# A fused attention and FFN kernel: two preparations moved behind the start of the FFN, one batch's RMS regrouped, and the last output tile split

## The chip, the cores and the metric

The kernel runs on one core of one Trainium2 chip. A core has a matrix engine (TensorE, PE in the profile), a vector engine (VectorE, DVE), a scalar engine (ScalarE, ACT), a general engine (GpSimd, POOL), and a queue engine (SyncE, SP) that mostly issues DMAs. Each engine has an instruction queue of its own; semaphores order them. The metric is the device time of one execution in microseconds, and of several executions the median.

## What is computed

Attention with routing by clusters feeds a gated FFN. Cut to what matters:

```python
batch, n_heads, seq, head_dim = (4, 8, 768, 64)      # 16 clusters a head
q_assign = argmax(q_n @ c_n.T); k_assign = argmax(k_n @ c_n.T)
mask   = q_assign[:, None] == k_assign[None, :]
scores = where(mask, q @ k.T / sqrt(D), -1e9)
attn   = softmax(scores) @ v                          # 4 x 8 x 768 x 64
x   = attn.transpose(0, 2, 1, 3).reshape(3072, 512)
xn  = x / sqrt(mean(x * x) + 1e-6) * rms_g
out = (silu(xn @ w_gate) * (xn @ w_val)) @ w_out      # d_ff = 1536
```

The FFN works on tokens, and a token's 512 features come from all eight heads of a batch. So the FFN of a batch can begin once the attention of its last head is done.

## The kernel before

**Slots, steps and pairs.** A slot is one head of one batch; there are 32. The scores of a slot are 768 x 768, held with keys on partitions, and are made in 9 steps of 512 columns (`NCH`), so the attention is a loop of 288 steps. Slots 8b to 8b+7 are batch b. Two neighbouring heads form a pair; there are 16, and pair p is used from step 18p on.

**Preparation of a pair** (`prep_parts`) has 13 parts, each put at a step by a table: four transpose groups on PE (`t_group`, three fp32 transposes each, copied from PSUM to `qk32` by DVE or by ACT), casts into the operand `aug` on POOL (`casts`), the product with the centroids on PE (`assign`), five DVE instructions that make a one-hot mask from it (`oh_tr` to `oh_back`), four small DMAs on SP that put the mask rows into `aug` (`place`), and a cast of v on POOL (`casts_v`). The mask rows make the scores of other clusters very negative, so no mask is applied later. `aug` and the cast v have three sets of buffers. The tables count from `base`, which for most pairs is step 18(p-2): there pair p-3, whose set pair p takes, has been used up, and pair p's own slots begin 36 steps later.

**Scores, exp, PV.** `score_chunk` makes the scores on PE and ACT takes the exp into `pT`. Before the FFN begins (the wide stage) one chunk is three steps long: 1536 columns, one exp, two PSUM buffers of three banks. Afterwards a chunk is one step of 512 columns. The PV product of a slot (`pv_group`, six groups of six matmuls) follows in steps 2 to 7 of the next slot. It accumulates in one PSUM buffer, `acc`. In step 8 of that slot `pv_norm` divides by the sums on DVE and writes the head's columns of `x`. The next slot's PV can't begin before.

**RMS of a batch** (`rms_parts`) has 14 parts for a batch's two halves of three token tiles each: the sums of squares of three tiles (`sumsq`, on ACT or on DVE, tile `jk`), the inverse root on POOL (`inv`, tile `ir`), the scaling of three tiles on DVE (`norm`, tile `xn`), and with the last of these a transposing DMA on SP into `xnT`. The parts' steps are counted from 72(b+1), the first step after batch b's last slot.

**The FFN** (`ffn_piece`) is cut into pieces, one to a step: of each unit of 128 hidden columns a gate product (`gp`, L382, then tanh on ACT and a product on DVE), a value product (`vp`, L382, then `gvT` on DVE) and, from the second half of a batch on, a quarter of an output tile (`dp`, L411: three matmuls of 512 columns; after four of them the eviction `ob`, L417 or L419, and the store). `LAG` is the number of steps by which the FFN of a batch starts behind the batch's last slot. After step 288 come `LAG` steps with FFN pieces and the rest of the last head, and then FFN pieces alone, with evictions on ACT.

**Order.** It is written out by hand: nothing reorders an engine's instructions. In each step the code emits the score chunk, one FFN piece, the evictions still pending but one, the PV group or the normalisation, and then the extras of that step: first the RMS parts, then preparation parts, loads and weight loads, as `at` registered them.

```python
for step in range(NT):
    score_chunk(slot, j)
    ffn_next(...)
    flush(1)
    if slot > 0 and 2 <= j < 2 + ST:
        pv_group(slot - 1, j - 2)
    if slot > 0 and j == 2 + ST:
        pv_norm(slot - 1)
    extras(step)
```

Of the kernel before, what the change touches and what calls it, by code (L numbers as in the profile page):

```python
# [8 lines left out]
F32 = mybir.dt.float32  # L9
# [10 lines left out]
def kernel(  # L20
# [12 lines left out]
    nc = tc.nc  # L33
    B, H, S, D = q.shape
    NC = centroids.shape[1]
    DM, DF = moe_w_gate.shape
    P = 128
# [3 lines left out]
    FC = DF // P  # L41
# [3 lines left out]
    NCH = ST * S // CH  # L45
# [7 lines left out]
    out_v = out.rearrange("(b p t) d -> b p t d", b=B, t=ST)  # L53
# [7 lines left out]
    ffn = ctx.enter_context(tc.tile_pool(name="ffn", bufs=2))  # L61
# [6 lines left out]
    wide = ExitStack()  # L68
    WCH = 3
    late = {}  # L70
    LAG = 33
    FFN0 = H * NCH + LAG

    ctx.enter_context(tc.manual_schedule())
# [12 lines left out]
    def load_pair(pi):  # L87
        for kind in range(3):
            load_part(pi, kind)
# [65 lines left out]
    wo = const.tile([P, FC, DM], BF16, name="wo")  # L155
# [25 lines left out]
    def prep_parts(pi):  # L181
        st = pi % NSET
        qk32 = [None]
        state = {}

        def t_group(g):
            a, side = divmod(g, 2)
            if g == 0:
                qk32[0] = prep.tile([P, 4, HS], F32, name="qk32", tag="qk32")
            tp = t_tile("tp")  # L190
            src = loads[pi][side]
            for i in range(TH):
                nc.tensor.transpose(tp[:, i * P:(i + 1) * P], src[:, a, i * P:(i + 1) * P], ident_f)  # L193
            dst = qk32[0][:, g, :]
            on_dve = (g % 2 == 0 if pi == 0 else g > 0 if pi == 1 else pi < 9 or g % 2)
            if on_dve:
                nc.vector.tensor_copy(dst, tp)  # L197
            else:
                nc.scalar.copy(dst, tp)
            state[g] = tp  # L200

        def casts():
            if pi == 0:
                for g in range(4):
                    a, side = divmod(g, 2)
                    for par in range(2):
                        dst = aug[0][a][0:D, side, par * HS:(par + 1) * HS]
                        src = state[g][par * D:(par + 1) * D, :]
                        if g == 3:
                            nc.vector.tensor_copy(dst, src)  # L210
                        else:
                            nc.scalar.copy(dst, src)
                return
            for a in range(2):
                for par in range(2):
                    nc.gpsimd.tensor_copy(aug[st][a][0:D, :, par * HS:(par + 1) * HS],  # L216
                                          qk32[0][par * D:(par + 1) * D, 2 * a:2 * a + 2, :])

        def casts_v():
            v_in = loads[pi][2]  # L220
            nc.gpsimd.tensor_copy(vbf[st][:, :, :, 0:D],  # L221
                                  v_in[:, :, :].rearrange("p a (t d) -> p a t d", d=D))

        def assign():
            h0 = 2 * (pi % NP)
            sp = t_tile("sp")
            for j in range(4):
                side, a = divmod(j, 2)
                nc.tensor.matmul(sp[32 * j:32 * j + 32, :], lhsT=cbd[:, h0 + a, :, :].rearrange("p c r -> p (c r)"),  # L229
                                 rhs=qk32[0][:, 2 * a + side, :], start=True, stop=True,  # L230
                                 tile_position=(0, 32 * j))
            state["sp"] = sp

        def oh_tr():
            tr = prep.tile([P, HS], F32, name="tr", tag="tr")
            nc.vector.transpose(tr, state["sp"])
            state["tr"] = tr[:, :].rearrange("p (n c r) -> p n r c", c=NC, r=2)

        def oh_max():
            mx = small.tile([P, TH * 4, 2], F32, name="mx", tag="mx")  # L240
            nc.vector.tensor_reduce(mx, state["tr"], axis=AX, op=ALU.max)
            state["mx"] = mx

        def oh_cmp():
            oh = prep.tile([P, HS], BF16, name="oh", tag="oh")
            nc.vector.tensor_tensor(oh[:, :].rearrange("p (n c r) -> p n r c", c=NC, r=2), state["tr"],
                                    state["mx"].unsqueeze(3).to_broadcast([P, TH * 4, 2, NC]), op=ALU.is_ge)
            state["oh"] = oh

        def oh_scale():  # L250
            oh = state["oh"]
            nc.vector.tensor_scalar(oh[0:64, :], oh[0:64, :], scalar1=1.0, scalar2=MASK,
                                    op0=ALU.subtract, op1=ALU.mult)

        def oh_back():
            ohT = prep.tile([P, HS], BF16, name="ohT", tag="ohT")
            nc.vector.transpose(ohT, state["oh"])
            state["ohT"] = ohT

        def place():  # L260
            ohT = state["ohT"]
            for a in range(2):
                for side in range(2):
                    r = 32 * (2 * side + a)
                    eng = nc.sync
                    if pi == 0:
                        eng = nc.gpsimd if side else nc.scalar
                    elif pi == 1 and (a or side):
                        eng = nc.gpsimd
                    eng.dma_start(out=aug[st][a][D:KA, side, :].rearrange("c (r n) -> c r n", r=2),  # L270
                                  in_=ohT[r:r + 2 * NC, :])

        return [lambda: t_group(0), lambda: t_group(1), lambda: t_group(2), lambda: t_group(3), casts, assign, oh_tr, oh_max, oh_cmp, oh_scale, oh_back, place, casts_v]


# [51 lines left out]
    def rms_parts(b):  # L327
        st = {}

        def sumsq(t):  # L330
            m, tl = divmod(t, TH)
            if tl == 0:
                st["ss"] = small.tile([P, TH], F32, name="ss", tag="ss")
                st["jk"] = xp.tile([P, 2, DM], BF16, name="jk", tag="jk")
            if tl % 2 == 0:
                nc.scalar.activation(st["jk"][:, 0, :], x_t[b][:, t, :], ACT.Square,  # L336
                                     accum_out=st["ss"][:, tl:tl + 1])
            else:
                nc.vector.scalar_tensor_tensor(st["jk"][:, 1, :], x_t[b][:, t, :], 1.0, x_t[b][:, t, :],
                                               op0=ALU.mult, op1=ALU.mult, accum_out=st["ss"][:, tl:tl + 1])  # L340
# [26 lines left out]
    gvT = {}  # L367
# [3 lines left out]
    def ffn_piece(n, kind, tail, on_act):  # L371
# [27 lines left out]
        elif kind == 2 and half >= 1:  # L399
            hf = half - 1  # L400
            b, m = divmod(hf, 2)
            t = m * TH + fc // 4
            qd = fc % 4
            if qd == 0:
                pool, tag = (ps_pv, "acc") if tail and (fc // 4) % 2 else (late["d"], "d")
                cur["d"] = pool.tile([P, DM], F32, name="dp", tag=tag)
            dp = cur["d"]
            for i in range(3):
                f = qd * 3 + i
                tl = fc // 4  # L410
                nc.tensor.matmul(dp, lhsT=gvT[hf][:, f, tl * P:(tl + 1) * P], rhs=wo[:, f, :],  # L411
                                 start=(f == 0), stop=(f == FC - 1))
            if qd == 3:
                def after():
                    ob = ffn.tile([P, DM], F32, name="ob", tag="ob", bufs=3)
                    if on_act:
                        nc.scalar.activation(ob, dp, ACT.Copy, scale=0.5)  # L417
                    else:
                        nc.vector.tensor_scalar_mul(ob, dp, 0.5)  # L419
                    nc.sync.dma_start(out=out_v[b, :, t, :], in_=ob)  # L420
                pend.append(after)

    def flush(keep=0):
# [19 lines left out]
    def at(step, fn):  # L443
        extra.setdefault(step, []).append(fn)
# [24 lines left out]
    for b in range(B):  # L469
        steps = (9, 9, 10, 11, 12, 13, 15, 19, 19, 25, 26, 27, 28, 29)  # L470
        if b == 0:
            steps = (9, 9, 9, 14, 16, 18, 19, 20, 21, 21, 27, 30, 31, 33)
        for fn, step in zip(rms_parts(b), steps):
            at(H * NCH * (b + 1) + step, fn)
    for pi in range(2, B * NP):
        base = 2 * NCH * (pi - 2) + {2: 10, 3: 5}.get(pi, 0)
        if pi < 9:
            steps = (-8, -5, -3, 0, 1, 2, 4, 5, 6, 7, 9, 9, 10)
        else:
            steps = (-5, -4, -3, -2, 0, 1, 2, 3, 4, 5, 6, 6, 10)  # L480
        for fn, step in zip(prep_parts(pi), steps):
            at(base + step, fn)
        if pi < B * NP - 3:
            at({6: 100, 7: 106}.get(pi, base + 12), lambda pi=pi: load_pair(pi + 3))
    for i, step in enumerate((50, 58, 68, 76, 86, 94, 100, 105, 111, 117, 123, 129)):
        at(step, lambda i=i: w_load(i))
    def extras(step):
# [58 lines left out]
```

## Time and profile before

| what | value |
|---|---|
| time, median of 13 runs | 355.75 us (354.45 to 357.61) |
| the profiled execution | 357.09 us; its span 355.1 us |
| PE busy | 337.2 us, 95% of the span |
| weight loads (PEld) busy | 204.1 us |
| ACT busy | 224.7 us |
| DVE busy | 221.4 us |
| POOL busy | 87.0 us |
| chain that ended last | PE 77%, DVE 9%, ACT 5%, DMA 4% |
| mean of one wide exp (1536 columns) | 1453 ns, 35 of them |
| mean of one narrow exp (512 columns) | 597 ns, 183 of them |
| mean of one fp32 transpose | 287 ns, 192 of them |

The span is measured from the first to the last instruction of one profiled execution; the time of a run includes a little around it. A matmul's duration contains its latency, and matmuls overlap, so the spacing of their starts says what they cost, not their mean. In rows of the timeline the columns are start, duration, engine, line, operation, output and input tiles, and count; brackets give how long the engine was idle just before and what ended the wait. Rows of the windows view give the stretch and its length, then busy microseconds (and counts) of PE, weight loads, DVE, ACT and POOL, then the granted PE clock as a share of full speed, the share of the DMA engines and GB/s.

### The profile page before, as it was taken

To read this page: it belongs to the slowest core of one execution; us is meant where nothing else is said; L and a number is where in the kernel's file an instruction comes from. 1 tells how busy PE (TensorE), PEld (TensorE's weight loads), DVE (VectorE), ACT (ScalarE), POOL (GpSimd) and SP (SyncE) were. 2 spreads that over 40 slices of the span, in tenths; PEclk is the share of its full clock that TensorE was granted. 3 is DMA by queue.
4 is the path that set the end of the run, shared out by engine and by line. 5 is a ranking of instruction groups with operands and counts; after the bars stand their busy time and mean duration, and the time that the engine had idled before them with its cause. 6 is when DMAs were issued, how large, how long until landed. Compare 5 with 4: busy or idle time off the path is not lost.

```text
span 355.1 us, 7433 instructions
## 1 busy us (share of the span) xinstructions
PE 337.2 (95%) x2907; PEld 204.1 (57%) x2939; DVE 221.4 (62%) x449; ACT 224.7 (63%) x383; POOL 87.0 (25%) x122
## 2 busy tenths in 40 slices
PE   8888999799999999999999999999999999999995
PEld 3456666466656565556656565556666555555542
DVE  4657667867575678757474668855545687555630
ACT  3487888787778687767667687767775442323321
POOL 2674565763332123230311224200000110000000
PEclk9999999879999999999999999999999999999999
DMA  7466799689954053071400013130000053000012
GB/s 263 150 196 185 222 224 225 92 125 293 266 128 142 4 173 74 20 202 38 137 35 8 31 41 47 42 74 31 2 30 32 30 77 75 31 30 30 31 59 89
DMA packets 38194, 35.38 MB, mean 100 GB/s; under 512 B 15072, under 2 KB 34960, under 8 KB 38160
## 3 DMA queue, kind: packets, MB, share of 16 engines
q1 hardware_dynamic: 31936, 29.98, 28.0%
q0 software_dynamic: 5984, 4.84, 9.7%
q8 instruction: 23, 0.38, 0.4%
q10 hardware_dynamic: 240, 0.08, 0.1%
q14 instruction: 11, 0.09, 0.1%
HBM read 28.61 MB, written 6.29 MB: 98 GB/s over the span
## 4 chain that ended last, share of the span: by engine, by line
PE 77%; DVE 9%; ACT 5%; DMA 4%; issue 3%; POOL 1%; POOLq 0%; SPq 0%; DVEq 0%; ACTq 0%
PE gp L382 15%; PE vp L382 15%; PE dp L411 15%; PE sc L297 10%; PE acc L311 8%; PE tp L193 5%; PE scw L297 5%; PE sp L229 3%; DVE xn L353 2%; ACT pT L300 2%; DVE qk L197 2%; DMA aug<-ohT 2%; DMA q_in<-in_q_dram 1%; DMA k_in<-in_k_dram 1%; ACT jk L336 1%
## 5 line engine op out<-in xcount | busy, mean ns | idle before, releaser
L300 ACT ACTIVATE pT<-sc 128x512 bf16<-128x512 f32 x183 | 108.0, 597 | 44.4 <-PE sc L297 43.5
L391 DVE SCALAR_TENSOR_TENSOR uu<-th,gp 128x384 f32<-128x384 f32 x96 | 53.0, 552 | 61.8 <-ACT th L387 61.8
L382 PE MATMUL vp<-xnT,wv 128*128 128x384 bf16 x384 | 78.1, 325 | 1.5 <-DVE gvT L397 1.4
L387 ACT ACTIVATE th<-gp 128x384 f32<-128x384 f32 x96 | 47.1, 491 | 49.2 <-PE gp L382 45.0
L382 PE MATMUL gp<-xnT,wg 128*128 128x384 bf16 x384 | 78.1, 325 | 0.0
L311 PEld LDWEIGHTS <-pT 128*128 128x128 bf16 x1152 | 58.5, 98 | 27.3 <-DVE x L321 2.9
L411 PE MATMUL dp<-wo,gvT 128*128 128x512 bf16 x257 | 69.8, 378 | 3.1 <-ACT ob L417 1.5
L297 PE MATMUL sc<-aug 80*128 80x512 bf16 x244 | 69.2, 327 | 0.8 <-ACT pT L300 0.8
L216 POOL CAST aug<-qk 64x768 bf16<-64x768 f32 x60 | 52.1, 868 | 62.0 <-DVE qk L197 51.3
L311 PE MATMUL acc<-vbf,pT 128*128 128x65 bf16 x1152 | 64.1, 195 | 1.9 <-DVE x L321 1.3
L300 ACT ACTIVATE pT<-scw 128x1536 bf16<-128x1536 f32 x35 | 48.9, 1453 | 15.4 <-PE scw L297 15.3
L397 DVE TENSOR_TENSOR gvT<-uu,vp 128x384 bf16<-128x384 f32 x96 | 52.6, 548 | 6.4 <-PE vp L382 0.9
L382 PEld LDWEIGHTS <-wg 128*128 128x128 bf16 x384 | 37.2, 97 | 30.8 <-issue 0.9
L382 PEld LDWEIGHTS <-wv 128*128 128x128 bf16 x384 | 37.1, 97 | 21.1 <-issue 2.6
L297 PEld LDWEIGHTS <-aug 80*128 80x128 bf16 x384 | 33.7, 99 | 22.6 <-issue 9.7
L411 PEld LDWEIGHTS <-gvT 128*128 128x128 bf16 x288 | 27.9, 98 | 27.3 <-issue 2.3
L197 DVE COPY qk<-tp 128x384 f32<-128x384 f32 x47 | 25.9, 554 | 24.7 <-PE tp L193 22.4
L297 PE MATMUL scw<-aug 80*128 80x512 bf16 (+1 forms) x140 | 30.2, 340 | 2.0 <-DMA aug<-ohT 1.4
L221 POOL CAST vbf<-v_in 128x768 bf16<-128x768 f32 x16 | 13.2, 825 | 46.8 <-issue 41.9
L353 DVE SCALAR_TENSOR_TENSOR xn<-x,ir,g_b 128x512 bf16<-128x512 bf16 x24 | 20.1, 850 | 6.6 <-POOL ir L345 6.6
L344 POOL TENSOR_SCALAR ir<-ss 128x3 f32<-128x3 f32 x8 | 1.6, 195 | 88.3 <-ACT jk L336 86.5
L321 DVE TENSOR_TENSOR x<-acc,inv 128x384 bf16<-128x384 f32 x32 | 17.8, 557 | 1.1
(54 smaller groups left out, 202.1 us busy)
## 6 DMA issues: line engine op xcount, KB each, us to landing
q_in<-in_q_dram SPq DMA_DIRECT2D x16, 384.0 KB, 4.6
k_in<-in_k_dram SPq DMA_DIRECT2D x16, 384.0 KB, 5.3
v_in<-in_v_dram SPq DMA_DIRECT2D x16, 384.0 KB, 5.8
out_dram<-ob SPq DMA_DIRECT2D x24, 256.0 KB, 2.0
wg<-in_moe_w_gate_dram POOLq DMA_DIRECT2D x4, 384.0 KB, 5.6
wv<-in_moe_w_val_dram POOLq DMA_DIRECT2D x4, 384.0 KB, 6.5
wo<-in_moe_w_out_dram POOLq DMA_DIRECT2D x4, 384.0 KB, 7.8
aug<-ohT SPq DMA_DIRECT2D x57, 24.0 KB, 2.2
```

Of the source, the lines that this page charges most:

```text
L197: nc.vector.tensor_copy(dst, tp)
L216: nc.gpsimd.tensor_copy(aug[st][a][0:D, :, par * HS:(par + 1) * HS], qk32[0][par * D:(par + 1) * D, 2 * a:2 * a + 2, :])
L297: nc.tensor.matmul(sc[:, o:o + n], lhsT=ag[:, 1, kc * P:(kc + 1) * P], rhs=ag[:, 0, qo:qo + n], start=True, stop=True)
L300: nc.scalar.activation(pts[slot][:, j * CH:(j + nch) * CH], sc[:, :nch * CH], ACT.Exp, scale=scale)
L311: nc.tensor.matmul(acc[:, TORD[g], :], lhsT=pts[slot][:, kc * S + g * P:kc * S + (g + 1) * P], rhs=vb[:, a, TORD[kc], :], start=(kc == 0), ...
L321: nc.vector.tensor_tensor(x_t[b][:, :, h * D:(h + 1) * D], acc[:, :, 0:D], inv.to_broadcast([P, ST, D]), op=ALU.mult)
L353: nc.vector.scalar_tensor_tensor(st["xn"][:, tl, :], x_t[b][:, t, :], st["ir"][:, tl:tl + 1], g_b, op0=ALU.mult, op1=ALU.mult)
L382: nc.tensor.matmul(pt[:, :HS], lhsT=w[:, dc, fc * P:(fc + 1) * P], rhs=xnT[b, m][:, :, dc, :], start=(dc == 0), stop=(dc == DC - 1))
L387: nc.scalar.activation(th, pt[:, :HS], ACT.Tanh, scale=0.5)
L391: nc.vector.scalar_tensor_tensor(uu, th, 1.0, pt[:, :HS], op0=ALU.add, op1=ALU.mult)
L397: nc.vector.tensor_tensor(gvT[half][:, fc, :], uu, pt[:, :HS], op=ALU.mult)
L411: nc.tensor.matmul(dp, lhsT=gvT[hf][:, f, tl * P:(tl + 1) * P], rhs=wo[:, f, :], start=(f == 0), stop=(f == FC - 1))
```

## The change

Four things are changed.

1. Pairs 7 and 8. Their preparation is moved: counted from the first transpose to `casts_v`, pair 7 goes from steps 82 to 100 to steps 102 to 117, and pair 8 from steps 100 to 118 to steps 109 to 124. They also take the tighter table of steps that pairs 9 and up have, and half of their PSUM copies go to ACT as those pairs' do. The loads of pair 10 go from step 106 to 118, those of pair 11 from 120 to 126.
2. RMS of batch 0. Its parts stood at steps 81 to 105 and now stand at steps 81 to 93. Of each half's three sums of squares two were on ACT and one on DVE; for batch 0 it is now one on ACT and two on DVE.
3. `LAG` goes from 33 to 30, so the FFN begins at step 102 instead of 105, the wide stage ends there, and three steps fewer follow the last slot.
4. The last output tile is made in two halves of 256 columns, each with its own PSUM buffer, eviction and store.

```diff
-    LAG = 33
+    LAG = 30
...
-            on_dve = (g % 2 == 0 if pi == 0 else g > 0 if pi == 1 else pi < 9 or g % 2)
+            on_dve = (g % 2 == 0 if pi == 0 else g > 0 if pi == 1 else pi < 7 or g % 2)
...
-            if tl % 2 == 0:
+            if tl == 2 or tl == 0 and b > 0:
                 nc.scalar.activation(st["jk"][:, 0, :], x_t[b][:, t, :], ACT.Square,
                                      accum_out=st["ss"][:, tl:tl + 1])
...
-            if qd == 0:
-                pool, tag = (ps_pv, "acc") if tail and (fc // 4) % 2 else (late["d"], "d")
+            tl = fc // 4
+
+            nh = 2 if n >= NU + FC - 4 else 1
+            qh, nq, N = qd * nh // 4, 4 // nh, DM // nh
+            if qd % nq == 0:
+                pool, tag = (ps_pv, "acc") if tail and (tl + qh) % 2 else (late["d"], "d")
                 cur["d"] = pool.tile([P, DM], F32, name="dp", tag=tag)
-            dp = cur["d"]
-            for i in range(3):
-                f = qd * 3 + i
-                tl = fc // 4
-                nc.tensor.matmul(dp, lhsT=gvT[hf][:, f, tl * P:(tl + 1) * P], rhs=wo[:, f, :],
+            dp = cur["d"][:, 0:N]
+            cols = slice(qh * N, (qh + 1) * N)
+            for i in range(3 * nh):
+                f = (qd % nq) * 3 * nh + i
+                nc.tensor.matmul(dp, lhsT=gvT[hf][:, f, tl * P:(tl + 1) * P], rhs=wo[:, f, cols],
                                  start=(f == 0), stop=(f == FC - 1))
-            if qd == 3:
+            if qd % nq == nq - 1:
...
-                    ob = ffn.tile([P, DM], F32, name="ob", tag="ob", bufs=3)
+                    ob = ffn.tile([P, DM], F32, name="ob", tag="ob", bufs=3)[:, 0:N]
...
-                    nc.sync.dma_start(out=out_v[b, :, t, :], in_=ob)
+                    nc.sync.dma_start(out=out_v[b, :, t, cols], in_=ob)
...
         if b == 0:
-            steps = (9, 9, 9, 14, 16, 18, 19, 20, 21, 21, 27, 30, 31, 33)
+            steps = (9, 9, 9, 10, 11, 12, 13, 14, 15, 16, 18, 19, 20, 21)
...
-        base = 2 * NCH * (pi - 2) + {2: 10, 3: 5}.get(pi, 0)
-        if pi < 9:
+        base = 2 * NCH * (pi - 2) + {2: 10, 3: 5, 7: 17, 8: 6}.get(pi, 0)
+        if pi < 7:
             steps = (-8, -5, -3, 0, 1, 2, 4, 5, 6, 7, 9, 9, 10)
         else:
             steps = (-5, -4, -3, -2, 0, 1, 2, 3, 4, 5, 6, 6, 10)
...
-            at({6: 100, 7: 106}.get(pi, base + 12), lambda pi=pi: load_pair(pi + 3))
+            at({6: 100, 7: 118}.get(pi, base + 12), lambda pi=pi: load_pair(pi + 3))
```

## The prediction

> **What bounds the kernel now.** I read the page's busy times first: PE is busy for 337.2 of 355.1 us, ACT 224.7, DVE 221.4, POOL 87.0. So the kernel is a PE queue, and what counts is where that queue stands still or runs at half clock. The windows of 10 us put the largest loss, after the start, between 60 and 80 us; in windows of 2 us:
>
> ```profile
> 62.00:64.00 2.00, 2.00 (x35) 1.63 (x32) 0.85 (x2) 1.97 (x6) 0.14 (x1) 1.00 0.62 99
> 64.00:66.00 2.00, 1.09 (x13) 0.78 (x12) 1.50 (x2) 2.00 (x2) 1.91 (x4) 1.00 0.23 53
> 66.00:68.00 2.00, 0.86 (x10) 0.49 (x8) 1.97 (x5) 2.00 (x3) 1.94 (x2) 0.98 0.74 55
> 68.00:70.00 2.00, 1.72 (x9) 0.33 (x10) 2.00 (x3) 0.39 (x2) 1.88 (x3) 0.50 0.92 142
> 70.00:72.00 2.00, 2.00 (x23) 1.48 (x22) 1.90 (x6) 0.78 (x1) 1.60 (x2) 0.50 0.92 175
> 72.00:74.00 2.00, 2.00 (x21) 1.33 (x19) 0.22 (x1) 1.79 (x4) 0.49 (x2) 0.50 0.82 80
> 74.00:76.00 2.00, 2.00 (x20) 1.38 (x18) 1.74 (x5) 1.77 (x2) 2.00 (x3) 0.82 0.91 139
> ```
>
> [...]PE works half of 64 to 68 us while DVE is full; then the clock is 0.50 until about 74.7 us. The timeline of this stretch says why (rows of DVE, POOL, PE and ACT):
>
> ```profile
> 60.66 0.69 DVE L339 SCALAR_TENSOR_TENSOR jk<-x 128x512 bf16<-128x512 bf16 x1
> ...
> 64.14 0.88 POOL L345 TENSOR_TENSOR ir<-ir,mhalf 128x3 f32<-128x3 f32 x1
> ...
> 65.06 1.34 DVE L353 SCALAR_TENSOR_TENSOR xn<-x,ir,g_b 128x512 bf16<-128x512 bf16 x1 [0.19 <-POOL ir L345]
> ...
> 66.54 0.56 DVE L321 TENSOR_TENSOR x<-acc,inv 128x384 bf16<-128x384 f32 x1
> ...
> 67.16 0.36 PE L311 MATMUL acc<-vbf,pT 128*128 128x65 bf16 x6 [0.66 <-DVE x L321]
> ...
> 71.22 1.45 ACT L300 ACTIVATE pT<-scw 128x1536 bf16<-128x1536 f32 x1 [2.83 <-PE scw L297]
> ...
> 75.17 2.79 ACT L300 ACTIVATE pT<-scw 128x1536 bf16<-128x1536 f32 x2 [0.23 <-PE scw L297]
> ...
> 78.22 0.81 PE L382 MATMUL gp<-xnT,wg 128*128 128x384 bf16 x4
> ```
>
> The RMS of batch 0 (jk, ir, xn) stands in the DVE queue ahead of the normalisation of slot 8 (66.54). There is one acc buffer, so the PV of slot 9 waits for it (67.16), the score chunk of step 93 queues behind that PV, and ACT is without an exp for 2.83 us. The first FFN matmul comes at 78.22, step 105. From there PE is full: 9.9 of 10 us in nearly every window.
>
> **What the Trainium skill says.** TensorE: Matmul & The Clock Gate, section Architectural detail: ACT and DVE queues are strict FIFO, and on PE only weight loads are pulled ahead. The rows above agree: slot 8's normalisation cannot pass xn. The same page, Part 1: PE falls to half rate after an idle window of about 3.4 us and recovers after a busy one. Here the means of 0.98 and 0.82 put half clock from 67.9 to 74.7 us, two such windows, and half activity was enough to bring it on. SBUF — State Buffer, section Terms: DVE and POOL take a shared port pair exclusively for a whole instruction. An xn of 1.34 us beside 0.74 us for the next one fits, though the trace doesn't prove it.
>
> **The change part by part.** "Step 102" and so on are the kernel's steps; all before step 81 is unchanged, so its times stand.
>
> *RMS of batch 0 (steps 81 to 93 instead of 81 to 105).* DVE's new order after slot 7's normalisation (done 60.63) is jk, jk, transpose of pair 6, xn, xn, xn, jk, jk, and only then slot 8's normalisation; after it xn x3. Only one Square of each half stays on ACT. DVE jk at a pitch of 0.62: 60.66, 61.28, done 61.9. ACT's Square stands behind the exp that ends at 62.40, as before, and is done at 63.0 (before, two were done at 63.77). From there to the first xn took 1.29 us (63.77 to 65.06): first xn at 64.3. Three xn at 0.70 and two jk at 0.62 are 3.35 us, the normalisation 0.78: done at 68.4, or 69.0 if one xn is again 0.6 slower. I take 68.8, so the PV of slot 9 starts at 68.9, where it started at 67.16. PE finishes what stands ahead of it (the chunk of step 90) at 65.3, since the exp of step 84 now ends at 64.3. So PE idles 3.6 us in one piece, and the clock must fall wherever its windows lie.
>
> *Pairs 7 and 8 leave the wide stage.* Before, PE filled part of its waits with their transposes. Now it has chunks and PV alone, and nothing gets ACT further: the step 93 chunk starts at 68.9 + 0.4 (six slow PV matmuls) = 69.3, before at 69.72. From that start the trace takes 1.5 us to the exp at 71.22 and 5.34 from there to the end of the step 99 exp (75.17 + 1.39 = 76.56). So 69.3 + 1.5 + 5.34 = 76.1 at this pace; without transposes, and if the clock recovers one window sooner, 75.2. If the clock never fell: 68.9 + 0.3 + 0.8 + three exps of 1.39 = 74.2. I take 75.8, bounds 74.2 and 77.0 (DVE ops slowed twice by POOL). The first FFN step waits for the last wide exp both times (78.01 before, after 77.96), so it is at 75.8: **2.2 us earlier**.
>
> *What PE must still do then.* The price of a pair's preparation beside the FFN is read from the gp matmuls, one per three steps:
>
> ```profile
> 84.27 0.81 PE L382 MATMUL gp<-xnT,wg 128*128 128x384 bf16 x4
> ...
> 91.44 0.81 PE L382 MATMUL gp<-xnT,wg 128*128 128x384 bf16 x4
> ...
> 97.71 0.81 PE L382 MATMUL gp<-xnT,wg 128*128 128x384 bf16 x4
> ...
> 101.40 0.81 PE L382 MATMUL gp<-xnT,wg 128*128 128x384 bf16 x4
> ```
>
> Nine steps without preparation take 91.44 - 84.27 = 7.17 us (2.39 per three). Nine with pair 9 take 9.96: a pair costs 2.8 us. Of this, 84.27 to 101.40 shows four transpose groups at 6.27 - 4.78 = 1.5, 0.37 each. Pair 7 moves whole (2.8); of pair 8 the two groups of steps 100 and 103 move (0.75, bounds 0.75 to 1.5, as the rest of pair 8 took 1.27 of 2.8 after 78.22). Steps 102 to 104 now have their scores and PV beside the FFN: 2.39 less gp and vp, which in the tail cost (306.85 - 297.12) / 5 - 0.65 = 1.30 us a pair; 1.1 us. Sum **+4.65**, of work that PE did in or beside its waits before. Fewer tail steps by three give nothing: the same FFN pieces run earlier in the same full PE queue.
>
> *Crowding.* Two preparations in steps 102 to 124 instead of one per 18. DVE's share at steps 109 to 113 comes to 5 x 0.37 (uu, gvT) + 2.5 (one-hot chain) + 1.1 (two copies), about 5.5 us, against about 5.5 of PE (5 x 0.8 + 4 x 0.37). Half of the two pairs' copies go to ACT, 0.48 each, which has 3 x 0.60 + 0.49 = 2.3 us of work in three steps of 2.39 plus 1.1 for three groups. I take +0.2, bounds 0 and 1.
>
> *Queues.* On SP the second input transposition (xnT, now step 93 instead of 105) and the loads of pair 9 (step 100) now stand ahead of pair 7's four aug copies (step 113, needed at 126); the loads of pair 10 go from 106 to 118, needed at 139, and land in about 5 us. On POOL the gate and value weight loads go ahead of pair 7's casts. Both cost nothing, with more than 10 us of slack each. FFN weights: the last value piece is issued at step 105, first used near 130.
>
> *Last tile in halves.* The chain ends with
>
> ```profile
> 351.35 0.60 ACT L417 ACTIVATE ob<-dp 128x512 f32<-128x512 f32 x1 [2.04 <-PE dp L411]
> ```
>
> and, in the windows view, the last store's data:
>
> ```profile
> 352.75:353.65 0.90, 0.00 (x0) 0.00 (x0) 0.00 (x0) 0.00 (x0) 0.00 (x0) 1.00 0.75 291
> ```
>
> Eviction of 512 columns takes 0.60; 384 columns (th) 0.49, so 256 about 0.39. The last store moves 291 GB/s for 0.9 us; half of it 0.45. Issue (0.8) and the 1.45 us after the data stay. PE's columns are the same; 24 matmuls of 256 for 12 of 512 cost nothing as long as the weight loads hide. **-0.55**, bounds -0.2 and -0.65.
>
> Sum: -2.2 + 4.65 + 0.2 - 0.55 = **+2.1 us**. The profiled execution took 357.09 us, its span and 2.0 around it; so 359.2 for such a one. It lies 1.3 above the median of 355.75, and I put the change on the median: **357.9 us**.
>
> **Rivals.**
> - *Faster, 353.9.* The DVE stretch does not hold up slot 8. With PE free, the wide stage is ACT's: seven exps of 1.39 (steps 81 to 99) and two Squares of about 0.65 end at 72.0 if the first starts at 61.0 as before; FFN 6.0 earlier, -6.0 + 4.65 - 0.55 = -1.9. It decides from where PV of slot 9 starts: the end of the stage is that start + 5.3 (warm) or + 6.9 (cold), and the break-even end is 78.0 - 4.65 + 0.35 = 73.7, so a start before 66.8 cold, 68.4 warm. For it: Square and ir come 0.8 us earlier than before. Against: five DVE operations in order after 64.3.
> - *No change, 355.5.* PE in the early FFN stage has room (9.47 busy in 90 to 100 us), and more preparation fills it: 2.3 of the 4.65 vanish. Against: pair 9 shows the full 2.8 there.
> - *Slower still, 360.5.* DVE falls behind with two preparations at once and gvT holds the vp buffers (PE waited 0.5 us for it at 99.2 already), five times over.
>
> **How the numbers follow.** Main case 0.60, own range 356.0 to 359.6 (from all low bounds together, +0.2, to most of the high ones, +3.8); faster 0.18; no change 0.12; slower still 0.10. About 0.3% (1.1 us) is what a measurement can tell from none. Faster takes its 0.18 and 0.02 of the others' edges: 0.20; same 0.12 and the low end of the main case, 0.16; slower 0.64. Range 353.8 to 360.2.
>
> **What would show it.** Right: slot 9's PV waits on x until about 69 us, PE clock 0.5 after it, first gp near 76, then gp spaced as around pair 9 twice between steps 102 and 124, last eviction about 0.4 us. Wrong: first gp before 73.5, no clock dip, or gp spacing under 3 us where pairs 7 and 8 are prepared.

## The result and the profile after

The changed kernel takes 361.44 us in the median of 11 runs (358.07 to 365.21), beside 356.33 us (354.39 to 359.05, 48 runs) for the kernel before on the same chip: a ratio of 1.0133 with an interval of 1.0109 to 1.0156. That is slower, as forecast, but 3.5 us more than the forecast and 1.2 us outside its range; 0.6 of the 3.5 us is the kernel before itself, taken as 355.75 in the forecast. The ratios and the table of runs below leave out every run over 1.5% above its kernel's fastest, called slow: of the changed kernel one, at 365.21 us. The profiled execution took 360.57 us, its span is 358.8.

The stretch where the RMS of batch 0 now stands, in the windows view of the kernel after (columns as before):

```profile
64.00:66.00 2.00, 1.63 (x35) 1.24 (x31) 0.58 (x3) 2.00 (x4) 0.64 (x2) 1.00 0.76 121
66.00:68.00 2.00, 0.81 (x4) 0.32 (x4) 1.52 (x2) 2.00 (x3) 2.00 (x3) 1.00 0.12 28
68.00:70.00 2.00, 0.00 (x0) 0.00 (x0) 1.97 (x5) 1.64 (x3) 0.01 (x1) 0.95 0.68 48
70.00:72.00 2.00, 0.80 (x8) 0.53 (x9) 1.31 (x5) 0.00 (x0) 1.31 (x3) 0.50 1.28 206
72.00:74.00 2.00, 2.00 (x23) 1.53 (x22) 1.87 (x3) 0.97 (x1) 2.00 (x3) 0.50 1.09 176
74.00:76.00 2.00, 2.00 (x17) 1.27 (x16) 0.04 (x1) 1.18 (x2) 0.04 (x1) 0.50 1.04 132
76.00:78.00 2.00, 1.23 (x10) 0.58 (x9) 0.71 (x2) 1.66 (x2) 0.00 (x0) 0.84 1.28 194
```

Before, PE worked half of the time from 64 to 68 us; now it does nothing at all from 68 to 70, while DVE is full. Half clock follows again. The timeline of the kernel after names the wait:

```profile
66.47 2.62 DVE L353 SCALAR_TENSOR_TENSOR xn<-x,ir,g_b 128x512 bf16<-128x512 bf16 x3 [1.89 <-POOL ir L345]
...
69.74 0.69 DVE L339 SCALAR_TENSOR_TENSOR jk<-x 128x512 bf16<-128x512 bf16 x1
...
70.58 0.56 DVE L321 TENSOR_TENSOR x<-acc,inv 128x384 bf16<-128x384 f32 x1
...
71.20 0.51 PE L311 MATMUL acc<-vbf,pT 128*128 128x65 bf16 x6 [3.78 <-DVE x L321]
...
73.03 1.45 ACT L300 ACTIVATE pT<-scw 128x1536 bf16<-128x1536 f32 x1 [3.39 <-PE scw L297]
...
78.80 0.81 PE L382 MATMUL gp<-xnT,wg 128*128 128x384 bf16 x4
...
354.33 0.39 ACT L421 ACTIVATE ob<-dp 128x256 f32<-128x256 f32 x1 [0.76 <-PE dp L415]
355.64 0.38 ACT L421 ACTIVATE ob<-dp 128x256 f32<-128x256 f32 x1 [0.92 <-PE dp L415]
```

Three xn and two jk pass ahead of slot 8's normalisation (70.58); the PV of slot 9 waits 3.78 us for it (0.66 before), and ACT is 3.39 us without an exp (2.83 before). The last two rows are the halved output tile.

This profile began badly: from 20 to 30 us its mean clock is 0.73, where the profile before has 1.00, and step 81, whose instructions up to there are unchanged, comes 2.00 us later. So times are best counted from the exp of step 81 (60.95 us before). The table cuts the rest of the span at the first tanh of the FFN, at the seventh, and at the last one in the trace; "half clock" counts stretches of 3.41 us at clock 0.50, before step 81 and then after it; what follows the last matmul of a span is not counted. Rows marked with a label are experiments told below.

| profile | half clock | to first tanh | to seventh | to last | to end | sum |
|---|---|---|---|---|---|---|
| before | 0, 2 | 18.13 | 16.45 | 245.87 | 13.70 | 294.15 |
| before_3 (same kernel) | 0, 0 | 16.18 | 16.44 | 245.89 | 13.71 | 292.22 |
| after | 2, 2 | 16.70 | 18.70 | 247.31 | 13.13 | 295.84 |
| after_3 (same kernel) | 0, 4 | 17.77 | 20.51 | 247.34 | 13.15 | 298.77 |
| warm | 0, 0 | 14.56 | 18.70 | 247.31 | 13.15 | 293.72 |
| norm_first | 0, 2 | 14.01 | 20.51 | 247.32 | 13.13 | 294.97 |
| norm_both | 1, 0 | 11.83 | 18.69 | 247.32 | 13.13 | 290.97 |
| only_rms | 0, 2 | 20.07 | 16.44 | 245.87 | 13.69 | 296.07 |
| no_rms | 0, 2 | 14.41 | 19.51 | 247.31 | 13.13 | 294.36 |
| pair7_wide | 0, 0 | 15.42 | 16.90 | 247.31 | 13.15 | 292.78 |
| both_warm | 0, 0 | 11.83 | 18.69 | 247.31 | 13.14 | 290.97 |

With two stretches after step 81 in each, the change costs 295.84 - 294.15 = 1.7 us. The other 3 us or so of the median are not in this pair of profiles. They are in how often the clock falls, which only many runs show.

### The profile page after: what moved, and what is told of

It is laid out like the page before. It is cut to its first block, busy times and chain, and to the rows that moved or that the text cites. A ratio compares the mean times of both kernels' runs of the same rounds, so it can differ in the third digit from the quotient of the medians.

```text
span 358.8 us, 7459 instructions
## 1 busy us (share of the span) xinstructions
PE 338.9 (94%) x2918; PEld 206.5 (58%) x2951; DVE 219.9 (61%) x449; ACT 225.8 (63%) x386; POOL 85.2 (24%) x122
## 4 chain that ended last, share of the span: by engine, by line
PE 85%; DVE 7%; ACT 3%; DMA 2%; issue 2%; POOL 1%; POOLq 0%; DVEq 0%; ACTq 0%
PE gp L382 17%; PE dp L415 17%; PE vp L382 16%; PE sc L297 11%; PE acc L311 9%; PE scw L297 6%; PE tp L193 5%; PE sp L229 3%; DVE qk L197 2%; ACT pT L300 2%; DVE xn L353 1%; DMA aug<-ohT 1%; ACT ob L421 1%; DVE x L321 1%; DMA c_in<-in_centroids_dram 1%
## 5 line engine op out<-in xcount | busy, mean ns | idle before, releaser
L300 ACT ACTIVATE pT<-sc 128x512 bf16<-128x512 f32 x186 | 109.9, 597 | 45.6 <-PE sc L297 44.7
L415 PE MATMUL dp<-wo,gvT 128*128 128x512 bf16 (+1 forms) x268 | 71.2, 369 | 3.6 <-ACT ob L421 1.9
L297 PE MATMUL sc<-aug 80*128 80x512 bf16 x248 | 70.3, 326 | 1.4 <-ACT pT L300 1.4
L216 POOL CAST aug<-qk 64x768 bf16<-64x768 f32 x60 | 50.3, 838 | 72.5 <-DVE qk L197 64.3
L300 ACT ACTIVATE pT<-scw 128x1536 bf16<-128x1536 f32 x34 | 47.9, 1455 | 18.9 <-PE scw L297 18.7
L415 PEld LDWEIGHTS <-gvT 128*128 128x128 bf16 x300 | 29.2, 98 | 27.1 <-issue 3.1
L197 DVE COPY qk<-tp 128x384 f32<-128x384 f32 x43 | 23.6, 555 | 26.3 <-PE tp L193 25.7
L297 PE MATMUL scw<-aug 80*128 80x512 bf16 (+1 forms) x136 | 31.5, 359 | 2.1 <-POOL ir L345 1.0
```

Source lines behind the costliest of these rows:

```text
L297: nc.tensor.matmul(sc[:, o:o + n], lhsT=ag[:, 1, kc * P:(kc + 1) * P], rhs=ag[:, 0, qo:qo + n], start=True, stop=True)
L300: nc.scalar.activation(pts[slot][:, j * CH:(j + nch) * CH], sc[:, :nch * CH], ACT.Exp, scale=scale)
```

## The experiments

**The same two kernels again.** No edit; two more profiles of each.

> The changed kernel once more. In the first pair of profiles the changed kernel was 3.7 us longer, and 2.0 of that came before step 81, where both run the same instructions; there the PE clock fell to half from 18.6 to 25.4 us in one profile and not in the other. Theory 1 (chance of the clock): this early dip falls on either kernel, so a new profile may lack it, and the change itself is worth about +1.7 us net of it. Theory 2 (the change is worth what the medians say): +4.7 us again, with at least 4 us of it after step 81. Theory 3: the early dip belongs to the changed program and is there again.

> The kernel before once more, against itself: a ratio of 1.000 within about 0.004. Theory 1: its profile has the early dip in some executions too, and is then about 2 us longer before step 81. Theory 3: never an early dip.

> A third look at the changed kernel, for one more profile. If the length of half clock after the wait makes its spread of 358.1 to 365.2 us: this run's time is about 356.7 us, plus 2 us for two stretches of half clock after the wait or 5 for four, plus 0.5 to 2 us if the early dip is there.

> A third look at the kernel before. One of its two profiles had half clock after step 84 (span 355.1), the other none (353.5). By the same account: a span of about 353.1, plus 1.6 us with half clock there, plus 0.5 to 2 us with the early dip.

The changed kernel: 360.38 us (4 runs, ratio 1.012, 1.0059 to 1.0181), and 361.35 in the single run, near the 361.7 expected of four stretches. The kernel before: 356.16 (20 runs, 0.9997, 0.9977 to 1.0016), and 355.31. Neither new profile of the kernel before has half clock before its last matmul: the dip at 68 us in the first profile is one case of several. The same part of the kernel in the windows view of before_3, at full clock:

```profile
66.59:70.00 3.41, 1.98 (x24) 0.94 (x24) 3.38 (x6) 1.93 (x3) 3.23 (x4) 1.00 0.97 115
70.00:73.42 3.42, 2.96 (x46) 2.10 (x42) 3.28 (x9) 3.36 (x5) 2.80 (x5) 1.00 0.83 120
```

Both new profiles of the kernel after have four stretches of half clock around the FFN's start. The early half clock of the first one is back, with one stretch, in after_again and not in after_3; none of the three profiles of the kernel before has it, so whether it falls on that kernel too is not shown. The windows view of after_3, cut at those stretches:

```profile
65.16:68.57 3.41, 0.11 (x1) 0.00 (x0) 3.34 (x9) 2.33 (x4) 0.81 (x2) 1.00 0.71 83
68.57:71.98 3.41, 2.92 (x29) 2.06 (x30) 2.51 (x4) 1.09 (x1) 3.25 (x5) 0.50 1.09 169
71.98:75.40 3.42, 3.42 (x26) 2.10 (x25) 0.75 (x2) 2.05 (x3) 0.00 (x0) 0.50 1.23 178
75.40:78.81 3.41, 2.15 (x12) 1.19 (x12) 0.00 (x0) 2.05 (x3) 0.00 (x0) 0.50 1.24 178
78.81:82.22 3.41, 3.41 (x20) 2.48 (x20) 0.55 (x1) 1.23 (x3) 0.00 (x0) 0.50 1.16 308
82.22:85.63 3.41, 3.41 (x39) 2.45 (x38) 2.10 (x5) 2.50 (x5) 2.06 (x3) 1.00 0.42 143
```

The row with 0.11 us of PE is the wait of slot 9's PV. Half clock then lasts until 82.2 us, well into the FFN, whose first matmuls stand in the timeline of after_3 with nearly twice the duration:

```profile
69.06 0.51 PE L311 MATMUL acc<-vbf,pT 128*128 128x65 bf16 x6 [3.79 <-DVE x L321]
...
77.04 1.49 PE L382 MATMUL gp<-xnT,wg 128*128 128x384 bf16 x4
...
83.12 0.81 PE L382 MATMUL gp<-xnT,wg 128*128 128x384 bf16 x4
```

Against the profile after with two stretches this costs 17.77 - 16.70 = 1.07 us before the first tanh and 20.51 - 18.70 = 1.81 from there to the seventh.

Every run comes with the mean clock granted over its span, timed runs too. A span of 355 us at a mean of 0.990 had 2 x 0.010 x 355 = 7.1 us at half clock, two stretches. Sorted by this count (the runs whose clock is on record; in brackets the number of runs, then their median time in us):

| kernel | 0 | 1 | 2 | 3 | 4 | 5 or 6 | mean count |
|---|---|---|---|---|---|---|---|
| before | (42) 355.2 | (40) 356.2 | (51) 356.8 | (2) 357.9 | (11) 359.3 | | 1.4 |
| after | | | (3) 358.1 | | (11) 361.3 | (2) 361.9 | 3.9 |
| warm | (11) 356.4 | (6) 358.0 | | (3) 360.3 | | | 0.8 |
| norm_first | | (4) 356.3 | (15) 357.4 | | (1) 359.7 | | 2.1 |
| norm_both | (5) 353.7 | (6) 355.6 | (5) 357.0 | (3) 357.2 | | | 1.4 |
| pair7_wide | (4) 355.3 | (1) 356.4 | (9) 358.0 | (2) 359.8 | (1) 360.3 | | 1.7 |
| only_rms | | | (4) 359.1 | | | | 2.1 |
| no_rms | | | (4) 357.3 | (3) 360.3 | (6) 358.5 | (3) 359.5, (1) 360.8 | 3.8 |
| refill | | | (4) 358.2 | (3) 359.6 | (4) 360.5 | | 3.1 |
| both_warm | (6) 354.4 | (1) 355.4 | | | | | 0.1 |

At an equal count the changed kernel is 1.3 us (two stretches, three runs) to 2.0 us (four) slower, which is the size of the forecast. But its count is 3.9 on average where that of the kernel before is 1.4. In the kernel before one stretch costs (356.8 - 355.2) / 2 = 0.8 to (359.3 - 356.8) / 2 = 1.25 us, so 2.5 more are 2.0 to 3.1 us. The means of these runs are 360.8 and 356.5, 4.3 apart: about 1.3 to 2.0 of work and waits, and the rest clock. The count is a coarse measure: it includes stretches early in the kernel, where nothing is changed, and where a stretch lies matters too (no_rms takes 360.3 us with three and 358.5 with four).

**warm: no idleness, the same wait.** Twenty matmuls of zeros are put in PE's queue before the PV that waits.

```diff
+    def stay_warm(n):
+        w2 = ps_t.tile([P, HS], F32, name="w2", tag="t")
+        for _ in range(n):
+            nc.tensor.matmul(w2, lhsT=zeros[:, 0:P], rhs=zeros[:, 0:HS], start=True, stop=True)
+    at(90, lambda: stay_warm(20))
```

> The changed kernel with 20 matmuls of zeros (384 columns) put into PE's wait at step 90; nothing reads their result. It leaves the wait and takes away the idleness. If the clock's fall is what makes the wait dear: clock 1.0 through the wide stage, exp of step 93 to exp of step 102 in 4.3 us instead of 6.0, total 1.5 to 3 us below the changed kernel. If the wait alone counts: within 0.5 us of the changed kernel.

357.04 us (20 runs), a ratio of 1.003 (1.0003 to 1.0056) to the kernel before, where the changed kernel had 1.0133. The chain on DVE is as long as ever: PV of slot 9 starts 8.26 us after step 81's exp, as in after_3. In the windows view of warm PE now works through the wait, and the clock holds:

```profile
66.00:68.00 2.00, 2.00 (x14) 1.17 (x13) 2.00 (x5) 1.96 (x4) 0.34 (x1) 1.00 0.51 43
68.00:70.00 2.00, 1.46 (x15) 0.74 (x13) 1.41 (x6) 0.00 (x0) 0.97 (x2) 1.00 1.22 185
70.00:72.00 2.00, 2.00 (x38) 1.58 (x36) 1.87 (x3) 1.42 (x2) 2.00 (x4) 1.00 1.30 192
```

Work that computes nothing takes 361.44 - 357.04 = 4.4 us off the median, or 3.3 against the 360.38 us that the changed kernel took on the same chip; 1.5 to 3 were expected. So most of the loss is the clock after the wait, not the wait. What is left, 293.72 against 292.22 in the table of stages, is the change without any half clock: +1.5 us (+1.2 by the runs: 356.4 and 355.2).

**refill: filling only before the FFN.** The changed kernel with `at(101, lambda: stay_warm(4))`, after the wait, so that the FFN may meet full clock.

> The changed kernel with 4 matmuls of zeros (384 columns) at step 101 alone: after the long wait, in the short one before the first narrow chunk (1.3 us), where PE waits for the last wide exp. Nothing reads them. The long wait at slot 9's PV stays. In the profiles so far the clock came back only after a stretch of 3.41 us that PE filled whole; stretches of 3.00, 3.33 and 2.23 busy us did not bring it back, and one changed run kept half clock for four of them, into the FFN. If that is the rule, half clock here lasts at most three, and the time falls by 1 to 2.5 us from the changed kernel (358.5 to 360.5). If the length of half clock has another cause: within 0.5 us of the changed kernel.

359.60 us (11 runs, 1.0074, 1.0042 to 1.0106): 1.8 us less than the changed kernel, with a mean count of 3.1 where it was 3.9. The time is as expected, but the rule behind it doesn't hold: in after_3 (71.98, above) half clock stayed after a stretch that PE filled whole, and in no_rms, told below, it ended after one with 3.21 us. A filler behind the dip doesn't prevent it; four runs in eleven still have four stretches. That it shortens the dip at times is the likely reading of the counts, and not shown: in the one profile the dip (66.38 to 73.21) is over before the filler.

**norm_first: the first half's RMS behind slot 8's normalisation.** Of the seven DVE instructions of this RMS that stood ahead of it, five (three xn, two jk) go behind it.

```diff
-            steps = (9, 9, 9, 10, 11, 12, 13, 14, 15, 16, 18, 19, 20, 21)
+            steps = (9, 9, 9, 10, 18, 18, 18, 19, 19, 19, 20, 21, 22, 23)
```

> The changed kernel with the RMS parts of batch 0 after the second pair of squares put one slot later, so that slot 8's normalisation stands directly behind the first two squares on DVE. If the DVE stretch ahead of that normalisation is what costs: PV of slot 9 starts about 3 to 4 us sooner after step 81, no clock dip there, first gp about 5 to 6 us sooner, total about 5 us below the changed kernel, at or 2 us below the kernel before. If the moved preparations are what costs: within 1 us of the changed kernel.

357.31 us (20 runs, 1.0034, 1.0017 to 1.0052). The timeline of norm_first shows where the wait went:

```profile
69.34 2.08 DVE L353 SCALAR_TENSOR_TENSOR xn<-x,ir,g_b 128x512 bf16<-128x512 bf16 x3 [1.35 <-POOL ir L345]
...
71.56 0.56 DVE L321 TENSOR_TENSOR x<-acc,inv 128x384 bf16<-128x384 f32 x1
...
72.26 0.49 PE L311 MATMUL acc<-vbf,pT 128*128 128x65 bf16 x6 [2.68 <-DVE x L321]
```

Slot 9's PV starts 4.30 us after step 81's exp without a wait (8.25 in the changed kernel), and that of slot 10 now waits 2.68 us, because the second half's xn stand ahead of slot 9's normalisation. Its profile still has two stretches of half clock (71.30 to 78.12), part of them in the FFN's first steps (20.51 to the seventh tanh). So the gain is 4.1 us instead of the 5 expected, and half clock is still there.

**norm_both: both halves behind a normalisation.** The second half's xn go to steps 99 to 101 as well, behind slot 9's normalisation.

```diff
-            steps = (9, 9, 9, 10, 11, 12, 13, 14, 15, 16, 18, 19, 20, 21)
+            steps = (9, 9, 9, 10, 18, 18, 18, 19, 19, 19, 20, 27, 28, 29)
```

> The changed kernel with both stretches of xn put behind the normalisations of slots 8 and 9, so neither PV waits for RMS work. In the run with only the first of them moved, PV of slot 10 waited 2.7 us for the second. If waits at PV make the idleness and this makes the half clock: no wait of PV for x over 0.5 us, exps of the wide stage back to back, no half clock, last wide exp about 4 us earlier than in the changed kernel, time 1.0 to 1.6% below the kernel before's median at best (about 351 to 352.5). If PE, having only chunks and PV here, falls to half clock anyway: 355 or more.

355.75 us (20 runs, 0.9971, 0.9944 to 0.9998): the same four changes but for these steps, and slightly faster than the kernel before, though not the 351 to 352.5 us that were hoped for. The ACT timeline of norm_both:

```profile
63.32 0.64 ACT L336 ACTIVATE jk<-x 128x512 bf16<-128x512 bf16 x1
63.84 0.21 ACT L336 ACTIVATION_READ_ACCUMULATOR jk<-x 128x1 f32 x1
63.93 4.14 ACT L300 ACTIVATE pT<-scw 128x1536 bf16<-128x1536 f32 x3
67.92 0.67 ACT L336 ACTIVATE jk<-x 128x512 bf16<-128x512 bf16 x1
68.44 0.24 ACT L336 ACTIVATION_READ_ACCUMULATOR jk<-x 128x1 f32 x1
68.53 4.17 ACT L300 ACTIVATE pT<-scw 128x1536 bf16<-128x1536 f32 x3
73.16 0.60 ACT L300 ACTIVATE pT<-sc 128x512 bf16<-128x512 f32 x1 [0.46 <-PE sc L297]
```

No row up to the last has a bracket: ACT goes from exp to exp, and the stage to the first tanh is 11.83 us, 4.35 less than in before_3. The count of half-clock stretches is 1.4, as before the change, so half clock is not gone: the profile has none in this stage, other runs have up to three somewhere. Without any, the kernel takes 353.7 us against 355.2.

**pair7_wide: pair 7 back in the wide stage.** norm_both's idea with pair 7's old table, copies and place; the RMS stands later to make room.

```diff
-            on_dve = (g % 2 == 0 if pi == 0 else g > 0 if pi == 1 else pi < 7 or g % 2)
+            on_dve = (g % 2 == 0 if pi == 0 else g > 0 if pi == 1 else pi < 8 or g % 2)
...
-            steps = (9, 9, 9, 10, 11, 12, 13, 14, 15, 16, 18, 19, 20, 21)
+            steps = (9, 9, 9, 10, 18, 18, 19, 32, 32, 33, 35, 38, 39, 40)
...
-        base = 2 * NCH * (pi - 2) + {2: 10, 3: 5, 7: 17, 8: 6}.get(pi, 0)
-        if pi < 7:
+        base = 2 * NCH * (pi - 2) + {2: 10, 3: 5, 8: 6}.get(pi, 0)
+        if pi < 8:
...
-            at({6: 100, 7: 118}.get(pi, base + 12), lambda pi=pi: load_pair(pi + 3))
+            at({6: 100, 7: 106}.get(pi, base + 12), lambda pi=pi: load_pair(pi + 3))
```

> A try at a better version: from the changed kernel, pair 7 goes back to where the kernel before prepares it, the first RMS half stands behind slot 8's normalisation, and the second RMS half comes after the FFN has begun (steps 104 to 112). Pair 8, the lag of 30 and the halved tile stay. PE then has pair 7's 2.8 us of work in the wide stage, where it waits for ACT, instead of in the FFN stage, where it does not: about 2 us below the run with both normalisations first, 350 to 352. If DVE, with pair 7's chain beside RMS, holds PV up again: 354 or more.

358.17 us (20 runs, 1.0038, 1.0009 to 1.0067), where 350 to 352 was hoped for. First to seventh tanh takes 1.79 us less than in norm_both: that is what pair 7 costs beside the FFN (a little more, if the RMS parts that now stand there cost anything). But the wide stage takes 3.6 us more. One row of its waits from 60 to 76 us (engine, what waited, on what, us, times, longest) and one of its timeline stand for it:

```profile
PE sp L229 <- DVE qk L197: 2.5, 1, 2.5
...
70.39 2.79 ACT L300 ACTIVATE pT<-scw 128x1536 bf16<-128x1536 f32 x2 [3.44 <-PE scw L297]
```

The pair's centroid product waits for its copy, which stands behind two xn on DVE, and ACT is 3.44 us without an exp. So with these steps pair 7 is better outside the wide stage; another order of its parts was not tried.

**only_rms and no_rms: the change in two parts.** only_rms is the kernel before with the RMS edit alone; no_rms is the changed kernel with the old RMS steps and the old share of ACT.

```diff
# no_rms, against the changed kernel
-            if tl == 2 or tl == 0 and b > 0:
+            if tl % 2 == 0:
...
-            steps = (9, 9, 9, 10, 11, 12, 13, 14, 15, 16, 18, 19, 20, 21)
+            steps = (9, 9, 9, 14, 16, 18, 19, 20, 21, 21, 27, 30, 31, 33)
```

> The kernel before with the RMS edit alone; pairs 7 and 8 and the lag stay as before. If the stretch makes the loss: PV of slot 9 starts 2 us or more later than the kernel before has it, PE idle for most of one clock window, time 0.4 to 1.2% above the kernel before. If the stretch only hurts because the transposes of pair 7 have left PE: within 0.3%.

> The changed kernel with batch 0's RMS parts and its split of the squares as in the kernel before; pairs 7 and 8, the lag of 30 and the halved tile stay. If the DVE stretch ahead of slot 8's normalisation makes the loss: PV of slot 9 waits about 2 us less than the 3.8 us it waits now, half clock is shorter or gone, time at most 0.6% above the kernel before (median about 356 to 358.5). If moving the pairs and the lag makes it: still 1% or more above it.

only_rms: 359.06 us (4 runs, 1.0069, 1.0044 to 1.0094). no_rms: 358.66 (17 runs, 1.007, 1.0047 to 1.0092). Each part alone costs about half of the loss, by different ways. only_rms has 2.1 stretches (1.4 before) and is 2.2 us slower at an equal count: the PV of slot 9 starts 9.19 us after step 81's exp (6.21 before), and in the ACT timeline of only_rms two exps wait for scores:

```profile
69.70 1.45 ACT L300 ACTIVATE pT<-scw 128x1536 bf16<-128x1536 f32 x1 [3.09 <-PE scw L297]
...
73.98 1.45 ACT L300 ACTIVATE pT<-scw 128x1536 bf16<-128x1536 f32 x1 [2.83 <-PE scw L297]
```

no_rms is only 0.5 us slower at two stretches but has 3.8 of them. Its pairs, lag and last tile were not taken apart further. The windows view of no_rms, cut at its stretches:

```profile
63.25:66.66 3.41, 1.28 (x20) 0.67 (x17) 1.57 (x4) 3.41 (x5) 2.62 (x4) 1.00 0.16 30
66.66:70.07 3.41, 3.41 (x32) 2.34 (x32) 1.78 (x4) 3.41 (x5) 0.00 (x0) 0.50 1.16 143
70.07:73.48 3.41, 1.99 (x25) 1.10 (x24) 1.51 (x3) 3.12 (x4) 2.61 (x4) 1.00 1.30 245
73.48:76.90 3.42, 3.21 (x18) 1.98 (x17) 1.02 (x2) 1.55 (x4) 0.00 (x0) 0.50 1.08 333
76.90:80.31 3.41, 3.41 (x39) 2.66 (x38) 2.26 (x5) 2.42 (x6) 1.43 (x2) 1.00 1.30 203
```

PE is busy 1.28 us in the first stretch and 1.99 in the third, and both are followed by half clock. ACT is busy for all or nearly all of the first three stretches: its exps set the pace, PV of slot 9 waits only 0.40 us, PE's longest wait there is 1.73 us, and with the preparations gone PE has too little to do. So a wait as long as the 3.8 us of the changed kernel isn't needed for the clock to fall.

**both_warm: the best of these.** norm_both with five matmuls of zeros each at steps 88, 97 and 101, where PE has little to do, and four more before the first step (`keep_warm(19)` for 15).

> A try at a version that beats both: both normalisations first, as in the run that did so, and PE's remaining waits of the wide stage filled with matmuls of zeros (5 each at steps 88, 97 and 101; 19 for 15 before the first chunk). If half clock in some executions makes the spread of 353.3 to 359.1 us there: a median of 353 to 354.5, ratio 0.990 to 0.995. If the fillings hold PE up more than they save: 356 or more.

354.42 us (7 runs, 353.90 to 355.37), a ratio of 0.993 (0.9902 to 0.9958), as expected: faster than both kernels. Six of seven runs have no half clock, where norm_both has five of nineteen. Without any it takes 0.7 us more than norm_both (354.4 and 353.7). From step 81 on the two profiles take the same 290.97 us, so the matmuls at steps 88, 97 and 101 cost nothing there; the 0.7 us lies ahead of step 81 or in the chip (the kernel before, too, took 355.5 without half clock beside both_warm and 355.2 beside norm_both).

## Why the prediction was right in sign and wrong in size

The wait on DVE was forecast rightly. The step that failed is the end of the wide stage. It was put 2.2 us earlier than in the one profile before, which had half clock there; the two profiles of the kernel before without it reach the first tanh 0.5 to 1.6 us sooner than the three of the changed kernel.

- *DVE's new order.* Predicted: normalisation of slot 8 at 68.8, PV of slot 9 at 68.9, PE idle for 3.6 us. Measured: 71.20 in a profile that was 2.00 us late at step 81, so 69.2; 69.06 in after_3; waits of 3.78 and 3.79. Right. One group was dearer than taken: three xn that ran beside a cast on POOL took 2.62 us, not 2.1, and 2.08 beside DMA issues alone (69.34 in norm_first). SBUF — State Buffer, section Terms, would allow for that; which instruction held which was not tried.
- *End of the wide stage: the term that failed.* "I take 75.8, bounds 74.2 and 77.0", with the note "if the clock recovers one window sooner". With the 1.07 us from the first FFN step to its tanh that is 15.9 us from step 81's exp, 2.2 less than before. Measured: 16.70 with two stretches (1.43 less), 17.75 and 17.77 with four. Against before_3, which has none, that is 1.59 us later (17.77 and 16.18). The term held two silent assumptions: that half clock would be one or two stretches and over before the FFN, and that the dip of the one profile before belonged to that kernel. Of 16 runs of the changed kernel 13 had four or more, early ones included. Of the kernel before, only 64 of 146 had two or more.
- *No term for the clock inside the FFN.* In after_3 four stretches reach 5.2 us past its start (77.04 to 82.22), which adds 1.81 us up to the seventh tanh. The sum had no line for it, because the first gp was expected at full clock.
- *PE's moved work.* Predicted +4.65 and +0.2 for crowding. Measured without half clock: 18.70 - 16.44 = 2.26 to the seventh tanh and 247.31 - 245.89 = 1.42 after it, 3.7 in all. Pair 7 was read at 2.8 from the gp spacing around pair 9, and costs 1.79 (norm_both against pair7_wide). The rest is 3.7 - 1.8 = 1.9, predicted 0.75 + 1.1. The spacing around pair 9 held waits too, of which the prediction itself named one (0.5 us for gvT) without taking it off; the other half us is not explained. No crowding is seen: from the first to the seventh tanh, where both pairs are prepared, PE is busy for 18.70 of 18.70 us in warm and in norm_both. One gp spacing there (2.68 us, 82.39 to 85.07 in the profile after) is under the 3 us that the prediction had named as a sign of being wrong; the others with preparation in them are 3.2 to 3.7.
- *Tail.* Predicted -0.55; 13.13 to 13.15 for 13.70, so -0.56. The half evictions take 0.39 and 0.38, predicted 0.39.
- *The sum.* +2.1 was forecast for like against like, and like against like is +1.7 by the profiles, +1.3 to +2.0 by the runs. That it fits so well is in part luck, for two errors offset each other in it: the wide stage was put 0.8 us too short, the moved work 1.2 us too dear. The 2 to 3 us on top are the half-clock stretches that were counted as given.
- *Rivals.* "Faster, 353.9" said that it decides from the start of slot 9's PV, and norm_both is that case: the PV starts 4.3 us after step 81's exp, 65.3 in the clock of the profile before, and the first tanh follows at 72.8 there (the rival: 72.0 + 1.07). Against that profile, with its two stretches, norm_both is 3.2 us shorter (294.15 - 290.97) where the rival has 1.9; against before_3, without any, 1.25. Its break-even for a cold PE, a start at 66.8, is met by no_rms: start at 66.56, sum 294.36 against 294.15. "No change" had one part of it right: 1.2 of the 4.85 us of moved work and crowding did not appear, where it had 2.3. "Slower still, 360.5" is near the median by number only: its DVE crowding isn't there.

On the skill: TensorE: Matmul & The Clock Gate, Part 1, has the clock return after at least one busy window. Here it took one, two or four, and a stretch with PE busy for 3.42 of 3.42 us (after_3, 71.98) left it at half, while one with 3.21 (no_rms, 73.48) brought it back. The prediction took one as enough when it let the clock recover before the FFN.

## What to carry to other kernels

Where one engine's queue carries both a short instruction that frees a buffer for PE and a long run of deferrable ones, put the short one first: here the same instructions, a few steps later, turned 1.3% slower into 0.3% faster. Before taking one profile as the state of a kernel, read the granted clock of all its runs and compare kernels at an equal count of half-clock stretches and by how often they have them; a change of idle pattern shows in the second. If PE must wait or run thin, cheap filler matmuls ahead of the wait can be worth as much as a shorter wait (warm 1.003, norm_first 1.0034), and the best kernel here has both.

## What the hardware showed that was not expected

- In each profile the changes of the clock lie whole numbers of 3.41 us apart, on a grid: in the profile after 18.61, 25.44, 69.81 and 76.64, where 69.81 - 18.61 is fifteen such lengths. From one execution to the next the grid lies elsewhere. So the same thin stretch of work can be cut in different ways. In the first profile of the kernel before a cell of the grid (64.50 to 67.91) held 1.50 us of PE, and half clock followed; in before_3 (66.59 to 70.00) and before_again (65.75 to 69.16) the emptiest cell there held 1.98 us, and none did. The wait of 3.8 us in the changed kernel leaves a cell with 0.03 to 0.81 us in each of its three profiles, and all of its 16 runs have two stretches or more. This would explain why the kernel before loses its clock in some runs only. No run sets the place of the grid, so that is argued and not shown.
- Half clock follows stretches in which PE is far from idle: after 1.28 and 1.99 us of 3.41 in no_rms. In norm_both's wide stage the stretches hold 2.10 to 2.43 us, and none was followed by it. Busy time alone doesn't decide: a cell with 1.89 us (pair7_wide, 67.21) and one with 1.57 near the end (only_rms, 351.68) kept full clock. Where the limit lies is not settled.
- How long it lasts is not settled either. The two profiles with an almost empty stretch ahead (0.11 us of PE in after_3, 0.03 in after_again) stayed at half clock for four stretches, those with 0.69 to 1.5 us for one or two; that is an observation on few cases, not a rule.
- The time of the unchanged kernel goes with the number of such stretches: a median of 355.2 us with none and of 359.3 with four, 0.8 to 1.25 us for each.
